# The last 224 features of gate and up with x stationary, and their way to the partitions through 32x32 transposes and DRAM

## The chip, the cores and the metric

The kernel runs on one core of a Trainium2 chip. The metric is device time in microseconds for one execution. The engines are PE (TensorE: matmuls; PEld are its weight loads), DVE (VectorE), ACT (ScalarE), POOL (GpSimd) and SP (SyncE, which here issues all DMAs). One profiled execution gives the trace that the text reads.

## What is computed

For 2048 tokens x of width 512, in float32:

```python
g = sigmoid((x * gate_w).sum(-1, keepdims=True))
a = sliding_window_attention(x @ wqkv, heads=32, head_dim=16, window=256) @ wo
b = (sigmoid(x @ w_gate) * (x @ w_up)) @ w_down        # 1376 features
out = g * a + (1 - g) * b
```

The change touches `x @ w_gate` and `x @ w_up` for the last 224 of the 1376 features, and the sum in `g`, which is computed as one more column of the same products.

## The kernel before

Every product of float32 values is made of three fp32r matmuls: each operand is split into a high part (an ACT cast) and a low part (a DVE subtraction), and high x high, high x low and low x high are added up in PSUM. x lies transposed in SBUF for the whole first phase (`xh`, `xl`: 512 inputs as 4 blocks of 128 partitions, 2048 tokens along the row).

**First phase, up to about 582 us.** A loop over 128 units (8 head groups of 4 heads x 16 query blocks; `u`) runs attention: score matmuls for the row maxima (`s_part`, L305; DVE finds the maximum, L311), transposed scores (`st_part`, L351; ACT takes the exponential, L356; POOL masks), and the product with V (`pv_part`, L384). PE has time to fill between them, and fills it with projections and with gate and up. The gate and up work is a list of groups, `rest`. Before, one group is (feature chunk f, weight w, token chunk c): the weights of 128 features are stationary, 512 tokens move, 12 matmuls (4 input blocks x 3 products), and the result has features on partitions. There are 11 chunks (ten of 128, one of 96), 2 weights, 4 token chunks: 88 groups. The 96 features of the last chunk take the gate's vector along as a 97th column in w=0.

The groups are not issued one by one. `turns()` (L527) cuts each matmul into two row halves of 64 partitions: in one turn it issues half 0 of matmul t and half 1 of matmul t-18, usually of another group, side by side on PE. Three turns go behind each head's score matmuls. When the second half of a group is through, its `post` goes to the front of the list `acts`, one entry of which is issued with each head: before, `gu_post` (L476), an ACT copy from PSUM to a staging tile `sp` (L479), whose store to the DRAM tensor `gu_d` is queued in `later` and issued by SP in the next unit (L279). The PSUM tiles of gate, up and projections share three buffers (tag `misc`). The last three groups are kept back (`HOLD`) and issued whole, with all 128 rows, around the end of the loop.

**Second phase, from about 582 us.** Four slices of 512 tokens, 11 steps each (`steps`, one per feature chunk). `h_load` (L549) brings gate and up of a step back from DRAM to one of eight buffers, five steps ahead; `h_skew` (L554) applies the sigmoid (ACT, L564) and the product (DVE, L565) three steps ahead and the split into `hb` (L67, L68; four buffers) two steps ahead; PE multiplies by `w_down` (`pd`, L71 to L73, 12 matmuls a step). In between, attention's output is loaded (`o_load`, L719 and L720), scaled and split; at the end of a slice PE applies `wo` (`pa`), DVE adds both parts with the gate's weights (L777), and SP stores the rows (L780). `gsum`, the argument of the gate's sigmoid, is gathered from `gu_d` by one DMA (L691) between the phases.

The order on PE, ACT, SP and DVE is the order of the code. Of the lines themselves, the ones that the working needs most:

```python
def gu_post(f, c, w):
    ...
    nc.scalar.copy(t[0:width(f, w)], gp.pop((f, c, w))[0:width(f, w)])
    later.append((gu_d[w, f, 0:fw, c * CH:(c + 1) * CH], t[0:fw]))
```

Of the kernel before, what the change touches and what calls it, by code (L numbers as in the profile page):

```python
# [22 lines left out]
CH = 512  # L23
NC = T // CH
NB = T // P
F = 1376
FCH = [P] * (F // P) + ([F % P] if F % P else [])
NF = len(FCH)
VW = DH + 1
# [9 lines left out]
QB = 32  # L39
HOLD = 3  # L40
GAP = 3
SHIFT = 18
WD_LATE = {0: 8, 1: 9, 2: 10}
# [5 lines left out]
def gated_mix_kernel(  # L49
# [28 lines left out]
    gu_d = nc.dram_tensor("gu_scratch", (2, NF, P, T), F32, kind="Internal").ap()  # L78
# [40 lines left out]
    with ExitStack() as actx:  # L119
# [114 lines left out]
        def group_mm(pt, fw, wh, wl, c, k, half):  # L234
            d, w = divmod(k, 2) if k < 2 * ND else (k - 2 * ND, 2)
            r = slice(0, P) if half is None else slice(64 * half, 64 * half + 64)
            mm(pt[0:fw], (wl if w == 2 else wh)[r, d], (xl if w == 1 else xh)[r, d, c * CH:(c + 1) * CH],  # L237
               start=k == 0 and half != 1, stop=k == 3 * ND - 1 and half != 0,
               skip_group_check=half is not None)

        def proj_mm(s, k, half=None):
            g, c = divmod(s, NC)
            if s not in pj:
                pj[s] = ps.tile([P, CH], F32, tag="misc", name=f"pj{s}", bufs=3)
            group_mm(pj[s], P, *wq[g], c, k, half)
# [197 lines left out]
        def gu_half(raw, fw):  # L443
            return raw.rearrange("p (d f) -> p d f", d=ND)[:, :, 0:fw]

        def width(f, w):
            return FCH[f] + (f == NF - 1 and w == 0)

        raw_gu = {}

        def load_gu(f, w):
            raw_gu[f, w] = cpool.tile([P, D], F32, tag="draw", name=f"guraw{f}_{w}", bufs=2)
            src = wgu[f, w] if FCH[f] == P else wgu_tail[w, :, :, 0:width(f, w)]
            nc.sync.dma_start(gu_half(raw_gu[f, w], width(f, w)), src)
# [3 lines left out]
        def split_gu(f, w):  # L458
            fw = width(f, w)
            raw = gu_half(raw_gu.pop((f, w)), fw)  # L460
            hi, lo = gv[:, 0, w, :, 0:fw], gv[:, 1, w, :, 0:fw]
# [8 lines left out]
        def gu_mm(f, c, w, k, half=None):  # L470
            fw = width(f, w)
            if (f, c, w) not in gp:
                gp[f, c, w] = ps.tile([P, CH], F32, tag="misc", name=f"gu{f}_{c}_{w}", bufs=3)
            group_mm(gp[f, c, w], fw, gv[:, 0, w, :, 0:fw], gv[:, 1, w, :, 0:fw], c, k, half)

        def gu_post(f, c, w):  # L476
            fw = FCH[f]
            t = cpool.tile([P, CH], F32, tag="sp", name=f"sp{f}_{c}_{w}", bufs=4)
            nc.scalar.copy(t[0:width(f, w)], gp.pop((f, c, w))[0:width(f, w)])  # L479
            later.append((gu_d[w, f, 0:fw, c * CH:(c + 1) * CH], t[0:fw]))  # L480
            if width(f, w) > fw:
                later.append((gu_d[w, f, fw:fw + 1, c * CH:(c + 1) * CH], t[fw:fw + 1]))
            if f + 1 < NF and c == 0:
                load_gu(f + 1, w)

        def gu_next(f, c, w):
            if f + 1 < NF and c == NC - 1:
                split_gu(f + 1, w)

# [4 lines left out]
        def proj_out(s):  # L494
# [10 lines left out]
            for f in range(NF) for w in range(2) for c in range(NC)  # L505
# [43 lines left out]
        def h_load(n):  # L549
            c, f = steps[n]  # L550
            for w in range(2):
                nc.sync.dma_start(hv[0:FCH[f], n % 8, w], gu_d[w, f, 0:FCH[f], c * CH:(c + 1) * CH])
# [44 lines left out]
        for u in range(N):  # L597
# [20 lines left out]
            if WD <= u < WD + 16 and (u - WD) % 2 == 0:  # L618
                load_d((u - WD) // 2)
            s4 = {5: 5, 9: 6, U_LAST: NSTEP - 2, U_LAST + 1: NSTEP - 1}.get(u)  # L620
# [45 lines left out]
            if 0 <= u - LAG < NU:  # L666
                mask_p(u - LAG)
            if WD + 2 <= u < WD + 18 and (u - WD) % 2 == 0:
                acts.append(lambda f=(u - WD) // 2 - 1: split_d(f, True))
# [21 lines left out]
        nc.sync.dma_start(gsum, gu_d[0, NF - 1, FCH[NF - 1]].rearrange("(b p) -> p b", p=P))  # L691
# [95 lines left out]
def _layout(inputs):  # L787
# [7 lines left out]
    nf = F // P  # L795
    gu = np.stack([wg, wu]).reshape(2, ND, P, F)
    main = gu[..., :nf * P].reshape(2, ND, P, nf, P).transpose(3, 0, 2, 1, 4)
    tail = gu[..., nf * P:].transpose(0, 2, 1, 3)
    gate = np.asarray(inputs["gate_w"]).reshape(1, ND, P, 1).transpose(0, 2, 1, 3)
    tail = np.concatenate([tail, np.broadcast_to(gate, (2, P, ND, 1))], axis=3)  # L800
# [32 lines left out]
```

## Time and profile before

| | us |
|---|---|
| median of 3 runs | 753.11 (752.37 to 753.42) |
| the profiled execution | 751.81 |
| its span, first to last instruction | 750.1 |
| PE, PEld busy | 744.0, 581.5 |
| DVE, ACT busy | 482.0, 435.5 |
| POOL busy | 171.9 |
| DMA moved | 103.58 MB in 69959 packets |

The granted PE clock is full throughout. A row of the timeline has start, duration, engine, line, operation and output<-inputs; a row of the windows has the stretch, its length, then busy time and number of instructions of PE, PEld, DVE, ACT and POOL, the clock, the mean busy share of the 16 DMA engines and GB/s; a row of the groups has count, busy time, mean ns of one, and the engine's idle time ahead of it with what ended it.

### The profile page before, as it was taken

What the parts mean: (1) busy time and instruction counts of PE and PEld (TensorE: products, weight loads), DVE (VectorE), ACT (ScalarE), POOL (GpSimd) and SP (SyncE); (2) the same over time, 40 slices, a digit from 0 to 9 for tenths busy, and PEclk for the clock granted to TensorE, in tenths of its full rate; (3) what the DMA queues carried; (4) which work ended last, traced back from release to release, by engine and by line L of the source; (5) the groups of instructions that cost most, each with busy time, mean ns of one, the idle gap of its engine ahead of it and who ended that gap; (6) DMA issues with size and microseconds to landing.
All of it is one profiled execution on the core that took longest, in us unless ns stands there. A gap on an engine that the chain in (4) does not pass through costs nothing.

```text
span 750.1 us, 17420 instructions
## 1 busy us (share of the span) xinstructions
PE 744.0 (99%) x6180; PEld 581.5 (78%) x6180; DVE 482.0 (64%) x1455; ACT 435.5 (58%) x927; POOL 171.9 (23%) x256
## 2 busy tenths in 40 slices
PE   8999999999999999999999999999999999999997
PEld 6877777787777877778787787778866888888886
DVE  5346767776776766776677676677613776657371
ACT  6422666666676667666667666666656663525241
POOL 7000233233233233323323333332331000000000
PEclk9999999999999999999999999999999999999999
DMA  8340434426344353443543426443355967557451
GB/s 305 96 113 19 105 98 124 127 68 181 113 114 125 109 154 105 122 112 108 153 122 92 125 71 177 125 130 102 109 187 176 290 209 233 170 194 223 128 150 56
DMA packets 69959, 103.58 MB, mean 138 GB/s; under 512 B 19314, under 2 KB 29042, under 8 KB 69872
## 3 DMA queue, kind: packets, MB, share of 16 engines
q1 hardware_dynamic: 69872, 102.48, 46.3%
q8 instruction: 48, 0.79, 0.4%
q14 instruction: 39, 0.32, 0.2%
HBM read 45.26 MB, written 32.00 MB: 103 GB/s over the span
## 4 chain that ended last, share of the span: by engine, by line
PE 97%; DMA 1%; DVE 1%; issue 0%; SPq 0%; ACT 0%; DVEq 0%
PE gu L237 34%; PE pv L384 12%; PE pj L237 11%; PE s L305 7%; PE st L351 5%; PE pd L71 5%; PE pd L73 5%; PE pd L72 5%; PE vps L71 2%; PE pa L73 2%; PE pa L71 2%; PE pa L72 2%; PE vps L73 2%; PE vps L72 2%; DMA V<-in_xT_dram 1%; DVE junk L311 0%
## 5 line engine op out<-in xcount | busy, mean ns | idle before, releaser
L311 DVE CUSTOM_DVE_ANT_0 junk<-s,mask 128x384 f32<-128x384 f32 (+2 forms) x512 | 272.1, 531 | 140.1 <-PE s L305 78.2
L237 PE MATMUL gu<-xh,w 64*128 64x512 f32 (+2 forms) x1384 | 344.4, 392 | 0.0
L356 ACT ACTIVATE pt<-st 128x384 f32<-128x384 f32 (+2 forms) x512 | 242.4, 474 | 169.3 <-PE st L351 69.8
L237 PE MATMUL gu<-xl,w 64*128 64x512 f32 (+3 forms) x692 | 227.4, 392 | 0.0
L237 PEld LDWEIGHTS gu<-xh,w 64*128 64x128 f32 (+2 forms) x1384 | 190.1, 183 | 19.3 <-issue 0.4
L361 POOL TENSOR_SCALAR_AFFINE_SELECT pt<-pt 128x512 f32<-128x512 f32 x128 | 88.1, 688 | 382.3 <-ACT pt L356 382.3
L351 PE MATMUL st<-ring 64*128 64x384 f32 (+2 forms) x536 | 170.2, 332 | 0.0
L305 PE MATMUL s<-ring 64*128 64x384 f32 (+2 forms) x536 | 165.8, 332 | 0.1
L305 PEld LDWEIGHTS s<-ring 64*128 64x128 f32 x536 | 94.4, 184 | 39.3 <-DVE nm L321 12.9
L237 PEld LDWEIGHTS gu<-xl,w 64*128 64x128 f32 (+3 forms) x692 | 107.9, 183 | 5.7
L351 PEld LDWEIGHTS st<-ring 64*128 64x128 f32 x536 | 97.1, 184 | 12.2 <-issue 2.7
L237 PE MATMUL pj<-xh,wqh 64*128 64x512 f32 (+1 forms) x232 | 91.1, 397 | 0.3 <-ACT xh L67 0.2
L384 PE MATMUL pv<-pt,V 128*32 128x384 f32 (+2 forms) x1408 | 91.0, 388 | 0.0
L237 PE MATMUL pj<-xl,wqh 64*128 64x512 f32 (+1 forms) x232 | 90.1, 393 | 0.4 <-DVE xl L68 0.4
L366 POOL TENSOR_SCALAR_AFFINE_SELECT pt<-pt 128x512 f32<-128x512 f32 x112 | 74.2, 663 | 0.0
L237 PE MATMUL pj<-xh,wql 64*128 64x512 f32 (+1 forms) x232 | 70.9, 392 | 0.0
L71 PE MATMUL pd<-ring,hb 128*128 128x512 f32 (+1 forms) x176 | 69.3, 394 | 0.0
L73 PE MATMUL pd<-ring,hb 128*128 128x512 f32 (+1 forms) x176 | 68.9, 392 | 0.0
L72 PE MATMUL pd<-ring,hb 128*128 128x512 f32 (+1 forms) x176 | 68.4, 389 | 0.0
L384 PEld LDWEIGHTS pv<-pt,V 128*32 128x32 f32 x1408 | 37.2, 109 | 36.0 <-issue 29.7
L67 ACT CAST hb<-V 128x512 fp32r<-128x512 f32 (+1 forms) x44 | 27.4, 622 | 63.9 <-DVE V L565 51.4
L479 ACT COPY sp<-gu 128x512 f32<-128x512 f32 (+2 forms) x88 | 51.1, 582 | 2.0 <-PE gu L237 2.0
(74 smaller groups left out, 898.5 us busy)
## 6 DMA issues: line engine op xcount, KB each, us to landing
gu_scratch<-sp SPq DMA_DIRECT2D x80, 256.0 KB
V<-gu_scratch SPq DMA_DIRECT2D x80, 256.0 KB
ring<-sh SPq DMA_DIRECT2D x128, 128.0 KB
ring<-sl SPq DMA_DIRECT2D x64, 128.0 KB
guraw<-in_wgu_dram SPq DMA_DIRECT2D x20, 256.0 KB
V<-in_xT_dram SPq DMA_DIRECT2D x16, 256.0 KB
oT_scratch<-ob SPq DMA_DIRECT2D x128, 32.0 KB
xl<-oT_scratch SPq DMA_DIRECT2D x16, 256.0 KB
```

Of the source, the lines that this page charges most:

```text
L71: mm(ps, lh, rh, start=first, stop=False)
L72: mm(ps, lh, rl, start=False, stop=False)
L73: mm(ps, ll, rh, start=False, stop=last)
L237: mm(pt[0:fw], (wl if w == 2 else wh)[r, d], (xl if w == 1 else xh)[r, d, c * CH:(c + 1) * CH], start=k == 0 and half != 1, stop=k == 3 * ...
L305: mm(pt[:, (k - k0) * P:(e - k0) * P], lhsT, blk(g, k, hh, 1, e - k), start=k == k0, stop=e == i + 1, skip_group_check=True,)
L311: nc.vector.tensor_tensor_reduce(junk[:, 0:n], pt[:, 0:n], mask[:, 3 * P - n:], scale=1.0, scalar=NEG, op0=ALU.add, op1=ALU.max, accum_out ...
L351: mm(pt[:, (q - j) * P:(e - j) * P], lhsT, blk(g, q, hh, 0, e - q), start=q == j, stop=e == last, skip_group_check=True,)
L356: nc.scalar.activation(pts[u][:, hh, 0:n], pt[:, 0:n], AF.Exp, scale=SCALE)
L361: nc.gpsimd.affine_select(p[:, :, 0:P], p[:, :, 0:P], pattern=[[0, HG], [1, P]], compare_op=ALU.is_ge, fill=0.0, base=0, channel_multiplie ...
L366: nc.gpsimd.affine_select(p[:, :, 2 * P:], p[:, :, 2 * P:], pattern=[[0, HG], [-1, P]], compare_op=ALU.is_gt, fill=0.0, base=0, channel_mu ...
L384: mm(pv[32 * hh:32 * hh + 32, (q % 4) * P:(q % 4 + e - q) * P], V[:, j, h * VW:h * VW + 32], p[:, hh, (q - j) * P:(e - j) * P], start=Fals ...
L479: nc.scalar.copy(t[0:width(f, w)], gp.pop((f, c, w))[0:width(f, w)])
```

## The change

The last two chunks (128 + 96 features) are taken out of the old scheme. Their gate and up weights stand side by side: 224 gate columns, 224 up columns, the gate's vector and a column of zeros, 450 in all. For each of 16 blocks of 128 tokens, x of that block is stationary and the 450 columns move (`tail_mm`), 12 matmuls a block. So `rest` has 9 x 2 x 4 = 72 old groups and 16 new ones: 88 as before, in the same places of the order, and with the same halves, turns and three held groups.

The result has tokens on partitions. `tail_post` transposes its 448 columns in 32x32 blocks on DVE, from PSUM to the staging tile, copies the gate's column straight to `gsum` on DVE, and queues one store. After a block transpose, partition 32a+j, column 32k+t holds token 32a+t, feature 32k+j; the store writes rows of 32 floats (128 bytes) to `tail_d`, 128 x 14 rows in one DMA. `h_load` of steps 9 and 10 reads them back with one DMA for each 32 features and weight, 32 partitions x 16 rows of 128 bytes each: 8 DMAs for step 9 and 6 for step 10, where there were 2 and 2.

The new weights come in four loads of 128x450 (u = 112, 114, 116, 118) through the `wqraw` buffers and are split two units later each, into two buffers of the projection weights and two of the four `hb` buffers. The last two chunks' old loads and splits go, and so does the gather of `gsum`.

```diff
+        def tail_room():
+            for k in range(2):
+                tw.append([
+                    wq_pool.tile([P, ND, P], F32R, tag=t, name=f"tail_{t}{k}").rearrange("p d f -> p (d f)")
+                    for t in ("wqh", "wql")
+                ])
+            for k in range(2):
+                both = cpool.tile([P, CH2], F32R, tag="hb", name=f"tail_hb{k}", bufs=4)
+                tw.append([both[:, 0:CH], both[:, CH:]])
...
+        def tail_mm(b, k, half=None):
+            if b not in tp:
+                tp[b] = ps.tile([P, CH], F32, tag="misc", name=f"tp{b}", bufs=3)
+            d, w = divmod(k, 3)
+            r = slice(0, P) if half is None else slice(64 * half, 64 * half + 64)
+            mm(tp[b][:, 0:TW], (xl if w == 1 else xh)[r, d, b * P:(b + 1) * P], tw[d][int(w == 2)][r, 0:TW],
+               start=k == 0 and half != 1, stop=k == 3 * ND - 1 and half != 0,
+               skip_group_check=half is not None)
+
+        def tail_post(b):
+            t = cpool.tile([P, CH], F32, tag="sp", name=f"tt{b}", bufs=4)
+            nc.vector.transpose(t[:, 0:2 * TF], tp[b][:, 0:2 * TF])
+            nc.vector.tensor_copy(gsum[:, b:b + 1], tp.pop(b)[:, 2 * TF:2 * TF + 1])
+            later.append((
+                tail_d[:, b].rearrange("k p t -> p k t"),
+                t[:, 0:2 * TF].rearrange("p (k t) -> p k t", t=QB),
+            ))
...
-            for f in range(NF) for w in range(2) for c in range(NC)
+            for f in range(NFM) for w in range(2) for c in range(NC)
+        ] + [
+            (lambda k, h=None, b=b: tail_mm(b, k, h), lambda: None, lambda b=b: tail_post(b)) for b in range(NB)
         ]
...
             for w in range(2):
-                nc.sync.dma_start(hv[0:FCH[f], n % 8, w], gu_d[w, f, 0:FCH[f], c * CH:(c + 1) * CH])
+                if f < NFM:
+                    nc.sync.dma_start(hv[:, n % 8, w], gu_d[w, f, :, c * CH:(c + 1) * CH])
+                    continue
+                for k in range(FCH[f] // QB):
+                    src = tail_d[(w * TF + (f - NFM) * P) // QB + k, c * NC:(c + 1) * NC]
+                    nc.sync.dma_start(
+                        hv[k * QB:(k + 1) * QB, n % 8, w].rearrange("j (m t) -> j m t", t=QB),
+                        src.rearrange("b (a j) t -> j (b a) t", j=QB),
+                    )
...
-        nc.sync.dma_start(gsum, gu_d[0, NF - 1, FCH[NF - 1]].rearrange("(b p) -> p b", p=P))
```

More of the change, by code (lines that the diff above doesn't have):

```diff
@@ L480, in gu_post @@
[L480 to L483, printed above, removed]
+            nc.scalar.copy(t, gp.pop((f, c, w)))
+            later.append((gu_d[w, f, :, c * CH:(c + 1) * CH], t))
+            if f + 1 < NFM and c == 0:
                 load_gu(f + 1, w)
         def gu_next(f, c, w):
-            if f + 1 < NF and c == NC - 1:
+            if f + 1 < NFM and c == NC - 1:
@@ new lines, in tail_load, with tail_split @@
+        def tail_load(d):
+            raw_gu[d] = cpool.tile([P, D], F32, tag="wqraw", name=f"tailraw{d}", bufs=2)
+            nc.sync.dma_start(raw_gu[d][:, 0:TW], wgu_tail[d])
+        def tail_split(d):
+            raw = raw_gu.pop(d)[:, 0:TW]
+            hi, lo = (v[:, 0:TW] for v in tw[d])
+            nc.scalar.copy(hi, raw)
+            behind.append(lambda: nc.vector.tensor_tensor(lo, raw, hi.bitcast(F32), op=ALU.subtract))
+        def tail_mm(b, k, half=None):
[6 more added lines that the diff above has]
+               skip_group_check=half is not None)
@@ L619, in gated_mix_kernel @@
                 load_d((u - WD) // 2)
+            if u == TAIL:
+                tail_room()
+            if TAIL <= u < TAIL + 2 * ND and u % 2 == 0:
+                tail_load((u - TAIL) // 2)
             s4 = {5: 5, 9: 6, U_LAST: NSTEP - 2, U_LAST + 1: NSTEP - 1}.get(u)
```

43 lines of the change are left out of this document (21 added, 22 removed).

## The prediction

> **What bounds the kernel now.** I read the profile's first part (busy time of each engine) and the chain that ended last, then the windows around the place of the change, then the order of single instructions there.
>
> ```profile
> span 750.1 us, 17420 instructions
> PE 744.0 (99%) x6180; PEld 581.5 (78%) x6180; DVE 482.0 (64%) x1455; ACT 435.5 (58%) x927; POOL 171.9 (23%) x256
> PE 97%; DMA 1%; DVE 1%; issue 0%; SPq 0%; ACT 0%; DVEq 0%
> ```
>
> PE is busy for 744.0 of 750.1 us, and 97% of the chain is PE. A busy PE alone would not prove much, because the ends of matmuls are modelled; so the distance between starts has to show whether PE runs tightly.
>
> ```profile
> 407.06 0.33 PE L351 MATMUL st<-ring 64*128 64x384 f32 x1
> 407.06 0.33 PE L305 MATMUL s<-ring 64*128 64x384 f32 x1
> 407.23 0.39 PE L237 MATMUL gu<-xh,w 64*128 64x512 f32 x1
> 407.23 0.39 PE L237 MATMUL gu<-xl,w 64*128 64x512 f32 x1
> ...
> 407.93 0.34 PE L351 MATMUL st<-ring 64*128 64x384 f32 x1
> ```
>
> Between the `st` at 407.06 and the one at 407.93 stand one pair of 384 columns (0.17 us, two row halves side by side) and three pairs of 512 columns (0.70 us, 0.233 each). The starts follow the number of moving columns, with no hole. So what a matmul streams is paid for in full, and DVE, ACT and DMA are bounds only where they make PE wait. The windows show where they come near:
>
> ```profile
> 508.00:540.00 32.00, 32.00 (x335) 25.53 (x333) 22.34 (x77) 21.13 (x48) 9.79 (x15) 1.00 0.33 103
> 540.00:582.00 42.00, 42.00 (x356) 29.43 (x353) 11.23 (x19) 26.23 (x61) 10.13 (x16) 1.00 0.59 181
> 582.00:610.00 28.00, 28.00 (x124) 22.98 (x123) 24.50 (x43) 18.82 (x35) 0.00 (x0) 1.00 1.01 305
> 623.00:664.00 41.00, 41.00 (x181) 33.64 (x181) 24.90 (x42) 17.78 (x30) 0.00 (x0) 1.00 0.60 191
> ```
>
> The columns are PE, PEld, DVE, ACT, POOL, clock, DMA share, GB/s. The last 16 groups of gate and up run from about 508 to 582. DVE has 9.7 us free before 540 and plenty after it; at 582 to 610 (the first slice of the second phase) the DMA engines are full, and DVE is busy for 24.5 of 28 us.
>
> **Matmuls: the gain.** Before, the last two feature chunks take 2 chunks x 2 weights x 4 token chunks x 12 = 192 matmuls of 512 moving columns (a pair of row halves counts as one). After, 16 token blocks x 12 = 192 matmuls of 450 columns, with as many weight loads. The first 18 turns, whose other half still belongs to chunk 8, stay at the pace of 512; at the end 18 turns with one half alone gain, so 192 remains the count. The price of 62 columns comes from the starts: (0.233 - 0.17) / 128 = 0.49 ns a column. A second pair of rows gives less:
>
> ```profile
> 567.37 0.28 PE L351 MATMUL st<-ring 64*128 64x256 f32 x1
> 567.49 0.39 PE L237 MATMUL gu<-xh,w 64*96 64x512 f32 x1
> 567.72 0.39 PE L237 MATMUL gu<-xl,w 64*96 64x512 f32 x1
> ```
>
> A single 256 takes 0.12, a single 512 takes 0.23: 0.43 ns a column. So 62 columns are worth 27 to 30 ns; the second row crosses a shorter distance of unlike neighbours, and I take 27: 192 x 0.027 = **5.2 us saved**. The ends are 0 (if something else set the pace) and 192 x 0.0305 = 5.9. That weight loads could set the pace is ruled out as far as 0.17: the 384 pairs load two stationary operands of 128 columns each, as the new matmuls do. The Trainium skill (TensorE: Matmul & The Clock Gate, section "Wait — 56ns, not 53.3ns?") says that start-to-start is the columns over 2.4 GHz plus about 2.5 ns; by that 62 columns are 25.8 ns and the gain 5.0 us. The trace has 0.233 where that rule has 0.216, so its fixed part is larger here, and its slope a little smaller than my rows give.
>
> **DVE instead of ACT: the cost.** 16 ACT copies go, 16 DVE transposes of 128x448 and 16 DVE copies of one column come.
>
> ```profile
> L311 DVE CUSTOM_DVE_ANT_0 junk<-s,mask 128x384 f32<-128x384 f32 x448 | 249.4, 557 | 118.2 <-PE s L305 64.5 <-PE st L351 43.0 <-PE gu L237 0.2
> L479 ACT COPY sp<-gu 128x512 f32<-128x512 f32 x80 | 46.5, 581 | 0.0
> L727 DVE STREAM_SHUFFLE spare<-xh 128x512 f32<-128x512 f32 x16 | 11.7, 733 | 0.0
> L326 DVE STREAM_TRANSPOSE nt<-nm 128x32 f32<-128x32 f32 x32 | 6.8, 211 | 1.1
> L715 DVE TENSOR_SCALAR omg<-gs 128x16 f32<-128x16 f32 x1 | 0.2, 169 | 0.0
> ```
>
> No row has a wide transpose. Lower bound: one block, 0.21 us (L326); upper: 14 such instructions, 2.95 us. I take the line between L326 and the shuffle of 512, which also moves 32-row blocks: 211 + (733 - 211) x 416 / 480 = 663 ns; the copy of one column at most 169 ns: 0.83 us a block, 13.3 us in all. ACT loses 16 x 0.58 = 9.3 us, which buys nothing, since ACT is no bound there.
>
> How much of it PE sees: three PSUM buffers serve these groups, and the first matmul of group n waits until group n-3 has been read. By the order of the instructions this lies some seven turns behind: three of the 384 pairs and six new pairs, 3 x 0.17 + 6 x 0.206 = 1.75 us. Until 540 DVE must first take the maximum of the next score tile (0.56 + 0.08, beginning about 0.3 after its matmul), in one case a 0.27 memset too, then transpose and copy: 0.3 + 0.64 + 0.83 = 1.8 to 2.05 us. That is 0 to 0.3 us late for each of groups 1 to 3; group 0 has the PV matmuls in between, and from 540 on DVE has no maxima left. What queues behind a late transpose is the next maximum, and behind that the PE matmul that needs its score buffer. I put **0.5 us** on this. The ends are 0 and, with 2.95 us transposes, about 1.3 to 2.3 us for each of 13 groups, 25 us in all; near 0.66 is where the shuffle row lies.
>
> The four splits of the new weights replace four splits of the old ones on the same engines (0.6 us each), some 20 us earlier, where DVE idles a third of each step; nothing. Two of the four `hb` buffers now hold weights until the last group, so step 2 of the second phase can be split only from the phase's start. It is needed two steps (5.5 us) later and takes about 3 us with the last two transposes ahead of it: nothing.
>
> **DMA: the pieces of 128 bytes.** Each of 16 stores becomes 1792 packets of 128 B instead of 128 or 96 of 2 KB, and per slice 14 loads of 512 packets replace 4 loads. Two windows hold small packets nearly alone: the stores of the maxima (128 packets of 128 B, and 64 semaphore packets), and the gather of `gsum` (4 B each), which the change removes. The third is one 256 KB output store.
>
> ```profile
> DMA packets 192, 0.02 MB, mean 10 GB/s; under 512 B 192, under 2 KB 192, under 8 KB 192
> q1 hardware_dynamic: 192, 0.02, 7.8%
> ...
> DMA packets 1630, 0.03 MB, mean 33 GB/s; under 512 B 1617, under 2 KB 1617, under 8 KB 1630
> q1 hardware_dynamic: 1630, 0.03, 97.4%
> ...
> q1 hardware_dynamic: 144, 0.26, 53.7%
> ```
>
> 7.8% of 16 engines over 1.7 us is 2.1 us for 192 packets, 11 ns each; 97.4% over 1.0 us is 9.6 ns each; 53.7% over 1.3 us is 11.2 us, 0.70 us on each engine. So a new store takes about 1808 x 11 / 16 = 1.24 us of the engines against 0.70, every 3.5 to 4 us, in windows with shares of 0.33 and 0.59: hidden. A slice's 14 loads take 14 x 528 x 11 / 16 = 5.1 us against 4 x 0.70 = 2.8. No row reads 128 B pieces from HBM; the bounds are 5.5 ns (the 2 KB rate) and, from the 4 B reads, hardly over 10, and I keep three times as a rival.
>
> SP's queue is the tighter place:
>
> ```profile
> 584.18 0.45 SPq L691 DMA_DIRECT2D gsum<-gu_scratch  x1
> 584.68 2.97 SPq L552 DMA_DIRECT2D V<-gu_scratch  x2
> ...
> 596.09 2.50 SPq L552 DMA_DIRECT2D V<-gu_scratch  x4
> 598.95 0.38 SPq L719 DMA_DIRECT2D xl<-oT_scratch  x1
> ...
> 604.46 3.18 SPq L552 DMA_DIRECT2D V<-gu_scratch  x6
> 615.50 8.48 SPq L780 DMA_DIRECT2D out_dram<-spare  x4
> ...
> 632.39 1.74 SPq L552 DMA_DIRECT2D V<-gu_scratch  x4
> ...
> 640.50 3.05 SPq L552 DMA_DIRECT2D V<-gu_scratch  x6
> 656.64 8.49 SPq L780 DMA_DIRECT2D out_dram<-spare  x4
> ```
>
> The loads of the last two chunks are the x4 at 596.09 and 632.39. With 0.43 to 0.5 us an issue (1.74 / 4, and the 512-packet load of 0.38 plus its gap), 14 of them take 6.6 us: 4 to 5 us more in each slice. SP then idles less before the output stores (607.6 to 615.5 and 643.6 to 656.6), which hides it from the end. What moves back are the loads queued behind: `xl`, and the next slice's first steps. From the second slice on, PE's data stand ready several steps ahead. In the first they don't:
>
> ```profile
> 596.65 0.68 DVE L68 TENSOR_TENSOR hb<-V,hb 128x512 fp32r<-128x512 f32 x1
> ...
> 604.08 0.69 DVE L68 TENSOR_TENSOR hb<-V,hb 128x512 fp32r<-128x512 f32 x1
> ...
> 606.67 0.68 DVE L68 TENSOR_TENSOR hb<-V,hb 96x512 fp32r<-96x512 f32 x1
> ```
>
> These ready steps 6, 9 and 10. PE begins step n at 581.6 + 2.75 n (12 x 0.229), that is 598.1, 606.3 and 609.1: slack 0.8, 1.5 and 1.7 us. Step 9's eight loads end their issue 1.3 us later than its two did (4 x 0.63 before, 8 x 0.47 after), step 10's 4 us later, part of which the emptier DMA queue gives back. Against this, the `gsum` gather goes; after it the next load took until 587.7 for two issues, some 2 us more than usual, though the two last stores will now hold SP for part of that. I put 0.5 us on the first slice (ends 0, since PE doesn't wait there today, and 4).
>
> **Sum.** -5.2 + 0.5 + 0.5 = -4.2 us. The profiled execution took 751.81 with a span of 750.1; it would be 747.6. It lies 1.3 below the median of the runs shown, 753.1, for which the forecast is **748.9**.
>
> **Rivals.** (1) *DVE eats the gain.* Transposes near 1 us, or a longer wait in the queue, make PE late by about 1 us at each of groups 1 to 3 and cost another 1 us: -5.2 + 4 = about 752. For: DVE's maxima and the new work fill nearly all of a step before 540. Against: subtractions of 0.69 stand in the same queue today and leave no hole in PE's starts. (2) *Small pieces cost three times as much* (33 ns). This is the one that ends slower. A slice's loads take 15 us of the engines; in the first slice, where they are full, step 9 and 10 come some 12.5 - 1.6 = 11 us late, and in each other slice (14 x 1.1 us of issue and landing from 632.4, data wanted near 646) about 2: -5 + 11 + 6 = +12, about 765. It decides from about twice the 11 ns, where the first slice's stall equals the gain. Against it: the 11 and 9.6 ns above. The Trainium skill (DMA: Bandwidth & Descriptors, section "Rules for kernel authors") speaks against a transpose by a plain DMA with a rearranged pattern, 19 times slower than the transposing kind; no run here shows it, and here 128 B stay together. (3) *The matmuls don't get shorter*, because something beside the columns sets 0.23: then only the costs stay, 753 to 754. Against it stand 0.17 and 0.12.
>
> **Chances.** The forecast's case 0.72 (747.0 to 751.3), rival 1 0.11, rival 2 0.12 (anything from 753 up), rival 3 0.05. The range 747.0 to 753.0 leaves out most of 2 and 3 and the top of the gain. A measurement of this kernel can tell about 0.2%, 1.5 us. Faster than 751.6: 0.72 plus a part of rival 1, 0.75; within it: 0.12; slower than 754.6: 0.13.
>
> **What would show it.** Right: starts of the 450 matmuls 0.20 to 0.21 apart; transposes near 0.66; the first matmul of the second phase 4 to 5 us before 581.6; step distances of 2.75 after it. Wrong: PE idle before the first matmul of a group, released by a transpose (rival 1); ACT or DVE in steps 9 and 10 waiting for loads, with PE behind them (rival 2); pairs at 0.23 (rival 3).

## The result, and the profile after

The changed kernel takes 759.78 us (median of 6 runs, 759.41 to 760.72), the kernel before 752.74 beside it (6 runs). The ratio is 1.0093 [1.0079, 1.0107]: 7.0 us slower, where 4.2 us faster was forecast. The profiled execution took 759.82. Executions of one kernel differ by up to 5 us here, and a profile shows one of them, so its own time is given where it lies far from the median.

The first part, DMA totals and chain of the profile after:

```profile
span 758.0 us, 17531 instructions
...
PE 744.6 (98%) x6180; PEld 585.0 (77%) x6180; DVE 491.4 (65%) x1487; ACT 427.0 (56%) x911; POOL 171.2 (23%) x256
...
DMA packets 121519, 103.57 MB, mean 137 GB/s; under 512 B 74206, under 2 KB 84446, under 8 KB 121432
...
PE 91%; DMA 4%; DVE 2%; SPq 1%; ACT 1%; issue 1%; DVEq 0%; ACTq 0%
```

PE's busy time is hardly changed, but its share of the chain fell from 97 to 91%: DMA, DVE and SP have come into it. The number of packets grew from 69959 to 121519 for the same 103.6 MB. The windows say where; their columns are those of the prediction's:

```profile
508.00:540.00 32.00, 31.92 (x344) 26.80 (x340) 24.54 (x85) 19.57 (x45) 9.87 (x16) 1.00 0.38 94
540.00:577.00 37.00, 36.84 (x340) 28.79 (x338) 14.45 (x35) 19.19 (x46) 9.64 (x16) 1.00 0.84 189
577.00:610.00 33.00, 29.70 (x124) 22.61 (x123) 22.79 (x43) 16.53 (x30) 0.00 (x0) 1.00 0.83 206
610.00:620.00 10.00, 6.74 (x17) 4.65 (x17) 8.20 (x14) 6.20 (x12) 0.00 (x0) 0.66 0.80 265
620.00:664.00 44.00, 44.00 (x194) 36.15 (x193) 25.43 (x43) 19.14 (x34) 0.00 (x0) 1.00 0.64 178
```

Up to 577 and from 620 on PE is full. All of the loss lies from 577 to 620, in the first slice of the second phase; between 610 and 620 the granted clock, too, is down at 0.66. The first matmul of that phase stands on either side of it. After:

```profile
577.59 0.36 PE L512 MATMUL tp<-tail_hb,xh 128*128 128x450 f32 x1
577.79 0.39 PE L75 MATMUL pd<-ring,hb 128*128 128x512 f32 x1
```

Before:

```profile
581.44 0.40 PE L71 MATMUL pd<-ring,hb 128*128 128x512 f32 x1
```

So the first phase **did** become 3.65 us shorter. The first slice then takes 52.6 us instead of 41.2, **11.4 longer**; the three other slices keep their 41.2. -3.65 + 11.4 = +7.75, and the spans differ by 7.9. The starts of the steps of the first slice are normally 2.75 apart (the last, with `wo`, takes 13.68); after, steps 4 to 6 take 4.20, 3.79 and 3.29 (3.0 us too much), and steps 8 to 10 take 3.94, 6.81 and 16.85 (8.4 too much).

What SP issued meanwhile (rows of SP's queue; start, time in which the issues held SP, xcount issues):

```profile
580.85 1.31 SPq L737 DMA_DIRECT2D spare<-in_wo_dram  x3
...
582.74 2.73 SPq L284 DMA_DIRECT2D tail_scratch<-tt  x2
585.52 2.12 SPq L590 DMA_DIRECT2D V<-gu_scratch  x2
...
596.55 9.87 SPq L594 DMA_DIRECT2D V<-tail_scratch  x14
...
607.69 1.81 SPq L590 DMA_DIRECT2D V<-gu_scratch  x4
```

The 14 loads hold SP for 9.9 us where four held it for 2.5, and two stores of 1792 pieces hold it for 2.7. The first load of the *next* slice's step 0 stands behind them: it goes out at 607.69, against 600.08 before, 7.6 us later. Before:

```profile
600.08 2.39 SPq L552 DMA_DIRECT2D V<-gu_scratch  x4
```

That this matters to the present slice is seen on ACT,

```profile
609.04 0.62 ACT L71 CAST hb<-V 96x512 fp32r<-96x512 f32 x1 [1.53 <-DVE V L610]
612.37 0.63 ACT L609 ACTIVATE V<-V 128x512 f32<-128x512 f32 x1 [2.70 <-DMA V<-gu_scratch]
612.90 0.60 ACT L116 CAST ring<-wdraw 96x512 fp32r<-96x512 f32 x1
```

and on PE:

```profile
610.05 0.39 PE L77 MATMUL pd<-ring,hb 128*128 128x512 f32 x1
613.56 0.80 PE L75 MATMUL pd<-ring,hb 96*128 96x512 f32 x1 [3.12 <-ACT ring L116]
614.49 0.79 PE L76 MATMUL pd<-ring,hb 96*128 96x512 f32 x1
```

What PE waits for longest is the last chunk of `w_down` (the low part of step 10's own `h` is ready at 611.98). The chunk was issued at 592.46, but its split (L116) stands on ACT behind the sigmoid (L609) of the next slice's step 0, which waits for the load that SP issued behind the 14. After 3.5 us without a start the first matmul takes 0.80, and from 615.1 to about 619.4 the starts stand 0.43 apart, not 0.23.

The stretch before 577, for the steps of the prediction. Starts of the 450-column pairs (one row half each):

```profile
528.93 0.36 PE L512 MATMUL tp<-tail_wqh,xh 64*128 64x450 f32 x1
...
529.13 0.36 PE L512 MATMUL tp<-tail_wqh,xl 64*128 64x450 f32 x1
...
529.34 0.36 PE L512 MATMUL tp<-tail_wql,xh 64*128 64x450 f32 x1
```

They are 0.20 apart, and a step between two score matmuls takes 0.78 where it took 0.87: 0.09 for three matmuls, 30 ns each. All transposes and all one-column copies (smallest, median and largest of the 16 in ns), as the two lines' own views have them:

```profile
L518 DVE STREAM_TRANSPOSE tt<-tp x16: 616/644/650, 520.5 to 581.1; 128x448 f32<-128x448 f32 x16
```

```profile
L519 DVE COPY gsum<-tp x16: 118/119/122, 521.0 to 581.7; 128x1 f32<-128x1 f32 x16
```

And one of the places where a group waited for them, first DVE's rows, then PE's:

```profile
530.53 0.27 DVE L406 MEMSET pv<- 128x256 f32 x1
530.71 0.62 DVE L518 STREAM_TRANSPOSE tt<-tp 128x448 f32<-128x448 f32 x1
531.25 0.12 DVE L519 COPY gsum<-tp 128x1 f32<-128x1 f32 x1
```

```profile
531.10 0.33 PE L356 MATMUL st<-ring 64*128 64x384 f32 x1
...
531.52 0.44 PE L512 MATMUL tp<-tail_wqh,xh 64*128 64x450 f32 x1
```

The new group begins 0.41 after the score matmul, not 0.17, behind memset, transpose and copy.

### The profile page after: what moved, and what is told of

It reads as the page before. It is cut to its first block, busy times and chain, and to the rows that moved or that the text cites. A ratio compares the mean times of both kernels' runs of the same rounds, so it can differ in the third digit from the quotient of the medians.

```text
span 758.0 us, 17531 instructions
## 1 busy us (share of the span) xinstructions
PE 744.6 (98%) x6180; PEld 585.0 (77%) x6180; DVE 491.4 (65%) x1487; ACT 427.0 (56%) x911; POOL 171.2 (23%) x256
## 2 busy tenths in 40 slices
DMA packets 121519, 103.57 MB, mean 137 GB/s; under 512 B 74206, under 2 KB 84446, under 8 KB 121432
## 4 chain that ended last, share of the span: by engine, by line
PE 91%; DMA 4%; DVE 2%; SPq 1%; ACT 1%; issue 1%; DVEq 0%; ACTq 0%
PE gu L242 27%; PE pv L389 11%; PE pj L242 10%; PE s L310 8%; PE st L356 5%; PE tp L512 5%; PE pd L77 4%; PE pd L76 4%; PE pd L75 4%; PE vps L75 2%; PE pa L75 2%; PE pa L77 2%; PE pa L76 2%; PE vps L76 2%; PE vps L77 2%; DMA V<-in_xT_dram 1%
## 5 line engine op out<-in xcount | busy, mean ns | idle before, releaser
L242 PE MATMUL gu<-xh,w 64*128 64x512 f32 x1152 | 295.1, 392 | 0.0
L242 PE MATMUL gu<-xl,w 64*128 64x512 f32 x576 | 190.5, 392 | 0.0
L242 PEld LDWEIGHTS gu<-xh,w 64*128 64x128 f32 x1152 | 160.6, 184 | 14.5
L242 PEld LDWEIGHTS gu<-xl,w 64*128 64x128 f32 x576 | 90.6, 185 | 3.8
L75 PE MATMUL pd<-ring,hb 128*128 128x512 f32 (+1 forms) x176 | 70.6, 401 | 4.8 <-ACT ring L116 3.1
L77 PE MATMUL pd<-ring,hb 128*128 128x512 f32 (+1 forms) x176 | 70.4, 400 | 1.6 <-DVE hb L72 1.6
L76 PE MATMUL pd<-ring,hb 128*128 128x512 f32 (+1 forms) x176 | 69.6, 396 | 0.1
L242 PEld LDWEIGHTS pj<-xl,wqh 64*128 64x128 f32 (+1 forms) x232 | 42.4, 185 | 4.3 <-DVE xl L72 1.9
```

What stands on the lines that cost most here:

```text
L75: mm(ps, lh, rh, start=first, stop=False)
L76: mm(ps, lh, rl, start=False, stop=False)
L77: mm(ps, ll, rh, start=False, stop=last)
L242: mm(pt, (wl if w == 2 else wh)[r, d], (xl if w == 1 else xh)[r, d, c * CH:(c + 1) * CH], start=k == 0 and half != 1, stop=k == 3 * ND - 1 ...
```

## The experiments

The theory after the result (COUNT): SP's row of issues is what became late; 14 loads for 4, and stores whose many pieces hold the queue. Its rivals: the small pieces cost DMA engine time; PE itself comes too early for loads that cannot come earlier; and, for the missing part of the gain, VectorE or a smaller price of columns. "First slice" below is its excess over the 41.2 us of before, in the profiled execution, worked out from the starts of the `pd` matmuls; "phase one" is the time from the same hole in PE's starts near 506 to the first `pd` (before 75.46, after 71.80).

**1. Loads by whole rows.** The tail's loads are 4 DMAs of 2 KB rows in a slice; stores as in the change.

```diff
-                for k in range(FCH[f] // QB):
-                    src = tail_d[...]
-                    nc.sync.dma_start(hv[k * QB:(k + 1) * QB, n % 8, w]..., src...)
+                nc.sync.dma_start(hv[0:FCH[f], n % 8, w], flat[off:off + FCH[f] * CH]...)
```

> The changed kernel, but steps 9 and 10 load the same number of bytes of the scratch tensor as whole rows of 2 KB, one DMA for each weight (4 a slice in place of 14 of 128-byte pieces); which values arrive is not the feature order, so the output is not the reference's. Theory COUNT (SP issues 14 DMAs at about 0.5 us, and everything behind them comes late) and theory PIECES (packets of 128 bytes fill the DMA engines in a stretch where they are full already) both expect the 8.4 us of steps 8 to 10 of the first slice to go, and about 751.5 us. Theory EARLY (the first slice's loads can't come earlier with PE, so that the first phase's gain is lost there) expects the 3.0 us of steps 4 to 6 to stay. If both are wrong, it stays near 759.8.

Measured: 753.22, ratio 1.0007 [0.9997, 1.0016]; first slice +4.9: steps 4 to 6 still 2.5, steps 8 to 10 2.4. The loads are worth 6.6 us; the 2.5 of steps 4 to 6 have another source.

**2. Fourteen loads, but of rows.** 14 DMAs of 32 x 2 KB.

```diff
+                for k in range(FCH[f] // QB):
+                    nc.sync.dma_start(hv[k * QB:(k + 1) * QB, n % 8, w], flat[o:o + QB * CH]...)
```

> As the run with whole rows, but cut into 14 DMAs a slice (32 partitions, 2 KB each), so that the count is that of the changed kernel and the pieces are long; the values are again not in feature order. COUNT expects about the changed kernel, 757 to 760; PIECES expects 751 to 752, as with 4 DMAs.

Measured: 758.59, 1.0066 [1.0041, 1.0090]; first slice +10.0 (step 9 takes 6.72). With the pieces gone and the count kept, 5.4 of the 6.6 us are back, by the medians: count 5.4, pieces 1.2. The five times lie between 754.52 and 759.65, so the 1.2 is not clear of the scatter; that the count is the larger part is.

**3. Stores by rows as well.** Experiment 1 with each block stored as 128 rows of 1792 bytes.

```diff
-                tail_d[:, b].rearrange("k p t -> p k t"),
-                t[:, 0:2 * TF].rearrange("p (k t) -> p k t", t=QB),
+            later.append((flat[o:o + 2 * TF * P].rearrange("(p x) -> p x", x=2 * TF), t[:, 0:2 * TF]))
```

> As the run with whole rows, and the 16 stores too are rows (128 of 1792 bytes in place of 1792 of 128); values not in feature order. If the stores of small pieces held SP up at the end of the first phase, steps 4 to 6 of the first slice lose most of their 3.0 us: about 749. EARLY expects them to stay, 751 to 752.

Measured: 749.76, 0.9962 [0.9948, 0.9977]; first slice +1.6, steps 4 to 6 normal. SP at the end of the first phase with small stores (experiment 1):

```profile
579.75 1.31 SPq L735 DMA_DIRECT2D spare<-in_wo_dram  x3
...
581.64 3.21 SPq L284 DMA_DIRECT2D tail_scratch<-tt  x2
584.89 2.12 SPq L590 DMA_DIRECT2D V<-gu_scratch  x2
```

and with row stores:

```profile
578.81 1.31 SPq L734 DMA_DIRECT2D spare<-in_wo_dram  x3
...
581.37 0.92 SPq L284 DMA_DIRECT2D tail_scratch<-tt  x2
582.34 1.34 SPq L589 DMA_DIRECT2D V<-gu_scratch  x2
```

Two stores of 1792 pieces hold SP for 3.2 us, two of 128 pieces for 0.9, and step 5's loads go out 2.5 us earlier. This is what made steps 4 to 6 late: by 2.5 us in experiment 1, by 3.0 in the change. PE enters the second phase as early here (578.0) as in the changed kernel, so coming early is no cost of its own: that rival falls.

**4. The count alone, on the kernel before.** Its loads of steps 9 and 10 are cut into 14 DMAs of 32 rows of 2 KB; nothing else.

```diff
+                for k in range(FCH[f] // QB):
+                    nc.sync.dma_start(
+                        hv[k * QB:(k + 1) * QB, n % 8, w],
+                        gu_d[w, f, k * QB:(k + 1) * QB, c * CH:(c + 1) * CH],
+                    )
```

> The kernel before with one edit: the loads of steps 9 and 10 are cut into 14 DMAs of 32 partitions a slice, in rows of 2 KB as before. COUNT alone, without anything else of the change: the first slice has 1.5 us of slack at step 9, 14 issues take some 4 to 5 us more, so COUNT expects 3 to 8 us more, 756 to 761. PIECES and EARLY expect no difference, 752.7.

Measured: 758.05, 1.0071 [1.0052, 1.0090]; first slice +5.5. SP, then PE:

```profile
597.54 8.23 SPq L556 DMA_DIRECT2D V<-gu_scratch  x14
...
607.00 1.82 SPq L553 DMA_DIRECT2D V<-gu_scratch  x4
```

```profile
609.46 0.39 PE L73 MATMUL pd<-ring,hb 128*128 128x512 f32 x1
612.50 0.50 PE L71 MATMUL pd<-ring,hb 96*128 96x512 f32 x1 [2.65 <-ACT ring L111]
```

Ten more issues a slice, without any other part of the change, bring the same hole at the same place: PE waits for the split of `w_down`.

**5. The split ahead of the sigmoid.** The changed kernel with one order turned round on ACT and DVE.

```diff
+            if n in WD_SPLIT:
+                split_d(WD_SPLIT[n])
             h_skew(n)
             if n in WD_LATE:
                 load_d(WD_LATE[n])
-            if n in WD_SPLIT:
-                split_d(WD_SPLIT[n])
```

> The changed kernel with one thing turned round: in each step of the second phase the split of a w_down chunk (steps 4, 6 and 8) is issued ahead of that step's sigmoid and splits of h instead of behind them. The count of loads (14 in a slice) and the stores stay. Theory ORDER (the 3.5 us hole of PE ahead of step 10 is the w_down split of chunk 10, which stands on ACT behind a sigmoid that waits for a load queued behind the 14): the hole goes, with it the about 2 us of half clock after it; the split of h for step 10 still comes late, so step 9 is not normal; 754 to 756. Rival LOADS ALONE (step 10's own data come so late that PE would wait as long for them): 758.5 to 760. Steps 4 to 6 keep their 3 us in both.

Measured: 755.72, 1.0032 [1.0021, 1.0044]: by the medians some 4 us of the loss are this queueing, as ORDER had it. The profiled execution took 757.80 (the nine: 754.51 to 757.80), and its first slice is still +8.8. The hole ahead of step 10 is smaller in it, but not gone: a start-to-start of 1.9 us, now for DVE's half of the same split (L117), which stands behind work that waits for a load. Half clock follows it from 615.2 to 618.7.

```profile
613.00 0.50 PE L76 MATMUL pd<-ring,hb 96*128 96x512 f32 x1 [1.47 <-DVE ring L117]
```

The other waits of the slice (3.4 us) are for the splits of `h`, and so for the loads themselves.

**6. ACT copies in place of the transposes,** on experiment 3.

```diff
-            nc.vector.transpose(t[:, 0:2 * TF], tp[b][:, 0:2 * TF])
-            nc.vector.tensor_copy(gsum[:, b:b + 1], tp.pop(b)[:, 2 * TF:2 * TF + 1])
+            nc.scalar.copy(t[:, 0:TW], tp.pop(b)[:, 0:TW])
+            nc.scalar.copy(gsum[:, b:b + 1], t[:, 2 * TF:2 * TF + 1])
```

> The run with row stores and row loads (749.76, second phase from 578.0), with the 16 transposes of 128x448 and the 16 copies of one column on VectorE replaced by two ACT copies each from PSUM, as the kernel before has them; nothing is transposed, so the features go into the wrong places. Theory VECTORE IN THE WAY: the 1.5 us that are missing between the 5.2 us of shorter matmuls and the 3.65 us by which the second phase begins earlier are waits of groups for the transposes; with ACT copies the second phase begins near 576.5 and the time is 748.0 to 748.6. Rival SHORTER GAIN (62 columns are worth less than 27 ns, some 19 to 20): the second phase still begins at 577.8 to 578.2, and the time stays 749.5 to 750.

Measured: 748.88, 0.9939 [0.9927, 0.9951], but not by the expected way: phase one takes 72.40, no shorter than with transposes (71.84), and in the profiles what is gained is the 1.6 us of the first slice. Now `st` waits for an exponential four times (PE's waits from 505 to 577):

```profile
PE st L356 <- ACT pt L361: 1.0, 4, 0.3
```

VECTORE IN THE WAY falls as I put it: taking the work off DVE doesn't bring the 1.5 us, since ACT's queue then holds PE as often. SHORTER GAIN falls too, since 62 columns are worth 30 ns, not 20. In experiment 3 the first slice's 1.6 us are a wait at step 10 for DVE's half of the `w_down` split, which runs at 606.51 there and at 605.24 here, while PE came to the second phase 0.5 us earlier there. Why it runs later there, with `wo` loaded at 578.8 in both, stays open.

**7. The same 14 loads from POOL's queue.**

```diff
-                    nc.sync.dma_start(
+                    nc.gpsimd.dma_start(
                         hv[k * QB:(k + 1) * QB, n % 8, w].rearrange("j (m t) -> j m t", t=QB),
```

> The changed kernel with nothing but the queue of the 14 tail loads of a slice changed: POOL issues them instead of SP, with the same pieces of 128 bytes and the same count. Theory SP QUEUE (what was late was SP's row of issues, at most 8 at a time, and all loads behind the 14): the holes of steps 8 to 10 shrink from 8.4 us to at most those of the run with row loads (1.4 to 2.4); steps 4 to 6 stay 3 us late, since the stores are untouched: 753 to 755. Rival DMA ENGINES (14 loads with 7168 pieces are too much for the full DMA engines, whoever issues them): 758 or more. A third way is that POOL's issue of one such load takes much longer than SP's 0.45 us; then steps 9 and 10 come late for that, in this slice above all.

Measured: 757.73, 1.0051 [1.0033, 1.0069]. Steps 8 to 10 are 2.9 us late, not 8.4: same pieces, same count, another queue. But steps 4 to 6 are now 5.9 us late, not 3.0. POOL issues the first of the loads from 579.0 on, 17.6 us before SP had come to them in the changed kernel (596.55). So they are on the DMA engines together with `wo`, the last stores and the loads of step 5; SP's two stores hold it for 3.51 us,

```profile
583.00 3.51 SPq L284 DMA_DIRECT2D tail_scratch<-tt  x2
```

and the first load of step 5 lands at 592.5, not at 590.4. The theory is nearly right for steps 8 to 10 (at most 2.4 were expected) and wrong on the total: loads that go out early push back the ones that are wanted first.

**8. Stores in quarters, loads of rows.** Features lie in DRAM row by row: each block is stored by four DMAs of 32 partitions with pieces of 128 bytes, and loaded as before the change.

```diff
+            for a in range(P // QB):
+                o = b * P + a * QB
+                later.append((
+                    tail_d[:, o:o + QB].rearrange("(k j) t -> j k t", j=QB),
+                    t[a * QB:(a + 1) * QB, 0:2 * TF].rearrange("j (k t) -> j k t", t=QB),
+                ))
```

> The transposed features lie in DRAM feature by feature (448 rows of 2048 tokens): a token block is stored by four DMAs, one for each 32 partitions, each 32 x 14 rows of 128 bytes, and a step is loaded as before the change, by two DMAs of whole 2 KB rows. Theory COUNT ON SP: the loads take no time of their own any more, so the end of the first slice is as in the run with row loads (steps 8 to 10 near 3.6, 3.1, 14.9), and the last stores, now 4 DMAs instead of 1 for each block, hold SP at the end of the first phase at least as long as there (steps 4 to 6 late by 3 us or up to 2 more): 753 to 755.5. Rival FIRST PHASE (64 stores instead of 16 make SP late while attention still runs, and PE waits for staging tiles or for rows of the stack): the second phase begins later than 579.5, 756 or more.

Measured: 759.32, 1.0078 [1.0064, 1.0092]: a miss, as FIRST PHASE had it. Steps 8 to 10 lose only 1.1 us, but the 64 stores hold SP at the end of the first phase: a chunk of `w_down` goes out at 577.10 (the same one at 571.24 in the changed kernel), ACT waits 4.0 us for it, and PE behind ACT:

```profile
581.14 0.50 PE L75 MATMUL pd<-ring,hb 128*128 128x512 f32 x1 [3.63 <-ACT hb L71]
```

**9. Small stores not last.** Experiments 5 and 8 together, and the last four old groups put behind the 16 new ones (their weights are loaded 6 units earlier).

```diff
+        rest = rest[:-NB - NC] + rest[-NB:] + rest[-NB - NC:-NB]
```

> As the one with stores in quarters, and two more edits: the four last groups of the old kind (chunk 8, w=1) go behind the 16 new ones, so that the last stores of the first phase are single DMAs of 2 KB rows again (the new weights are loaded 6 units earlier for that), and the w_down splits stand ahead of the sigmoids. Theory COUNT ON SP: nothing of the first slice is late any more, the second phase begins near 578, all steps are 2.75 and 13.68: 748.5 to 750, below the kernel before. Rival FIRST PHASE: the 64 small stores cost PE time before 578, or the earlier weights wait for their buffers: 752 or more.

Measured: 752.13, 0.9988 [0.9978, 0.9998]; phase one 72.97, first slice +2.1. Better than both kernels, against the one before by a hair, but a miss: the time is what FIRST PHASE gave, and phase one has lost 1.2 us to the changed kernel. `wo` is loaded at 581.40, 2.6 us later than in experiment 3: SP is still late.

**10. All 64 quarters from POOL,** on experiment 9 (`nc.gpsimd.dma_start` in place of `later.append`).

> The reordered version (four last old groups behind the new ones, w_down splits first, features stored by quarters, whole rows loaded; 752.1), with its 64 quarter stores issued by POOL instead of SP. Theory SP QUEUE: SP is back to the issues of the kernel before at the end of the first phase, less the gather, so wo and the first loads come about 2.5 us earlier than in that run, steps 0, 6 and 8 are near 2.75, and the time is 749.0 to 750.5. Rival POOL IN THE WAY (64 issues on POOL delay its masks, or the stores land late): the second phase begins later than 579.5, 752 or more.

Measured: 753.83, 1.0007 [0.9991, 1.0022], a miss, as POOL IN THE WAY. The profiled execution took 756.95 (the twelve: 752.44 to 756.95). In it the first slice has no late step, but the second phase begins at 586.3; 6.8 us before it, from 571.4 to 578.2, run at half clock. At full clock it would begin near 583, an estimate from these two. POOL's groups from 510 to 590:

```profile
L524 POOL DMA_DIRECT2D tail_scratch<-tt x60 | 37.7, 635 | 10.7 <-DVE gsum L521 3.9 <-issue 3.0 <-DVE mx L316 1.6
L366 POOL TENSOR_SCALAR_AFFINE_SELECT pt<-pt 128x512 f32<-128x512 f32 x17 | 11.5, 675 | 1.2 <-ACT pt L361 1.2
```

An issue takes POOL 0.635 us, 38 us of it in all, and the masks behind them come late: PE waits 1.20 us for one at 571.26. SP's row is cured, and POOL's is in the way instead.

**11. Stores and loads of the change from POOL** (one store a block, 14 loads a slice, split first).

> The changed kernel's layout (one store of a block with pieces of 128 bytes, 14 loads a slice), order of groups as in the change, w_down splits first, with both the 16 stores and the 14 loads of a slice issued by POOL. Theory SP QUEUE: neither the stores nor the loads stand in SP's row; the second phase begins near 578, steps 4 to 6 are normal, 8 to 10 late by at most 2 us: 749.5 to 751.5. Rival DMA ENGINES: steps 8 to 10 still several us late, 754 or more.

Measured: 777.96, 1.0322 [1.0298, 1.0346], outside both expectations. POOL gets through one large store in some 6.6 us:

```profile
599.39 1.10 POOL L520 DMA_DIRECT2D tail_scratch<-tt  x1 [6.26 <-issue]
605.95 1.10 POOL L520 DMA_DIRECT2D tail_scratch<-tt  x1 [5.45 <-DVE spare L777]
```

so the loads behind them land late, and step 8 takes 16.1 us. The landings in the trace say what POOL waits for: its next issue begins 0.3 us after the store ahead of it has landed (605.65 and 605.95, 612.24 and 612.54). Small ones overlap: up to three loads of 512 pieces are under way at once.

**12. Only the last four blocks' quarters from POOL,** on experiment 8 with the split first.

```diff
+                if b < NB - NC:
+                    later.append((dst, src))
+                else:
+                    nc.gpsimd.dma_start(dst, src)
```

> The version with stores in quarters and whole rows loaded (759.3; order of groups as in the change), with the w_down splits ahead of the sigmoids, and the stores of the last four token blocks issued by POOL instead of SP; POOL's last mask comes before the first of these. In the run where POOL issued all 64, one issue took 0.63 us, the masks came late and the second phase began at 586.3, but no step after it was late. Theory SP QUEUE: with 16 of the 64 on POOL behind the masks, SP's row is shorter than before the change, the second phase begins at 577.5 to 578.5, no step is late: 747 to 749.5. Rival STILL LATE (the 48 stores before, or the POOL stores' landing, hold the loads of the first steps): steps 0 to 6 late by 2 us or more, 750.5 to 753.

Measured: 755.32, 1.0036 [1.0023, 1.0049]: a miss, and above the range of STILL LATE too. Steps 1 to 10 are normal, but the 48 stores before make SP late. A chunk of `w_down` that SP issued at 571.24 in the changed kernel goes out at 576.49 here and lands at 581.41. It

```profile
576.49 0.42 SPq L110 DMA_DIRECT2D wdraw<-in_wd_dram  x1
```

holds ACT,

```profile
581.44 0.62 ACT L116 CAST ring<-wdraw 128x512 fp32r<-128x512 f32 x1 [4.29 <-DMA wdraw<-in_wd_dram]
```

and through it step 0:

```profile
582.63 0.80 PE L75 MATMUL pd<-ring,hb 128*128 128x512 f32 x1 [4.76 <-ACT hb L71]
```

**13 and 14. One and two quarters of each block from POOL,** on experiment 9.

```diff
+                    nc.gpsimd if a >= 2 else nc.sync,
```

(In 13 the condition is `a == 3`.)

> The reordered version (752.1; stores by quarters, whole rows loaded, the four last old groups behind the new ones, w_down splits first), with one of the four quarter stores of each block issued by POOL, 16 of 64. In that run SP's row blocked twice for 1.1 us near 557 and 571 behind the stores, and the wo loads went out at 581.4 where the run with row stores and ACT copies had 578.8. Theory SP'S ROW BEFORE 575 sets when the second phase's loads start: with 16 issues of 0.5 us less on SP, wo is loaded 1 to 2 us earlier, the late steps 0, 6 and 8 lose 1 to 2 us in all: 750.3 to 751.3. Rival DMA ENGINES: the pieces of 128 bytes are the same, so wo and the late steps stay: 752 or more. POOL has room for one issue of 0.63 us between its masks; if it hasn't, the second phase begins later than 579.5.

> The same with two of the four quarter stores on POOL, 32 of 64. Theory SP'S ROW: SP has then no more issues than before the change; 749.3 to 750.5, unless POOL's masks come late (all 64 on POOL made the second phase begin at 586.3); then PE waits for masked tiles before 572 and the time is 751 to 753 in spite of an SP row that is on time. Rival DMA ENGINES: 752 or more with wo and the late steps as in the reordered version.

Measured: 750.49, 0.9956 [0.9939, 0.9972], and **749.45, 0.9947 [0.9930, 0.9964]**. In both profiles, every step of the second phase is at its 2.75 or 13.68. `wo` is loaded at 581.40 in experiment 9, at 578.63 with one quarter moved, and with two:

```profile
577.84 1.32 SPq L741 DMA_DIRECT2D spare<-in_wo_dram  x3
...
580.39 0.81 SPq L284 DMA_DIRECT2D gu_scratch<-sp  x2
```

The windows of the version with two quarters:

```profile
540.00:578.00 38.00, 37.84 (x338) 29.03 (x336) 13.85 (x30) 20.86 (x49) 19.52 (x32) 1.00 0.79 190
578.00:620.00 42.00, 42.00 (x186) 34.47 (x185) 31.14 (x55) 24.39 (x44) 0.00 (x0) 1.00 0.75 238
```

PE is full from 578 to 620. The second phase begins at 578.5; phase one takes 72.80, so 2.7 of the changed kernel's 3.65 us are kept. The pieces are the same as in experiment 9; only issues left SP. Theory SP'S ROW is borne out, and DMA ENGINES falls for what was left.

## Why the prediction was wrong, point by point

- **Matmuls, 5.2 us: right in kind, a little small.** 0.20 between starts, 30 ns a matmul instead of 27, so 192 x 0.030 = 5.8. The 25.8 ns of the Trainium skill's rule that the prediction named (TensorE: Matmul & The Clock Gate, section "Wait — 56ns, not 53.3ns?") is the farther one.
- **Transposes, 0.66 us: right** (0.644); the copy took 0.119, under its bound of 0.169.
- **Waits for them, 0.5 us: too small.** Phase one gained 3.65 of 5.8, so by difference waits took some 2.1 us; not each of them is located. One is shown above, by the mechanism named (memset, transpose, copy in one row). That they would end at 540 was wrong: PE's starts show the same 0.41 at 547.8 and 555.7, where DVE has a `w_down` split of 0.69 ahead of the transpose, and from 543 to 559 the gain is 0.58 us, half of what the pace of the 7 us before 527 would give. Experiment 6 speaks for the fixed order of two full queues as the cause, and not DVE alone: on ACT the same work costs PE as much.
- **The new weights' splits, nothing; the emptier ACT, nothing: no run speaks against it.**
- **The step that failed: "I put 0.5 us on the first slice (ends 0, since PE doesn't wait there today, and 4)".** It measured 11.4. The row was read rightly (14 issues, more in SP's row), and then priced by the two loads of steps 9 and 10 alone. Its own sum was off, too: step 9's two loads ended after 2 x 0.63 = 1.26 us of the row, not after 4 x 0.63, so eight of 0.47 end 2.5 us later, not 1.3, against a slack of 1.5. Three more things are missing in it. First, 14 issues held SP for 9.9 us, not 6.6: two of them took 1.77 and 1.38 us in place of 0.49, and three times the row stood, some 0.6 us in all, until an earlier DMA had landed (the issue of 598.39 began 0.02 us after the landing of the one eight before it, issued at 593.13). The issue of step 9's last load ended at 603.23, against 597.26 before. Secondly, "what moves back are the loads queued behind: `xl`, and the next slice's first steps" was taken to be harmless in this slice. But ACT takes its work in order, and the next slice's sigmoid stands ahead of this slice's last `w_down` split; experiment 5 puts about 4 us on that, half clock included. Thirdly, the prediction saw that "the two last stores will now hold SP for part of that" and charged nothing for it; experiment 3 shows 3.5 us for small stores against rows.
- **Rival 2 named the place and the sign, with the wrong mechanism.** A piece of 128 bytes took 13 to 14 ns of a DMA engine on average (the packets of the changed kernel from 520 to 576 and from 582 to 610), near the 11 of the sum and far from this rival's 33. The pieces are 1.2 us of the 6.6, not clear of the scatter (experiment 2); the count on one queue is the rest, and the count alone, on the old kernel, costs 5.2 us (experiment 4). The other slices lost nothing, against the 6 us that this rival put on them.
- **Rival 1 was half right, rival 3 is out.** The waits behind DVE took some 2.1 of the 4 us of rival 1, but with transposes of 0.644 us, and they leave a gain; the matmuls did get shorter.
- **The gain was real.** With the queue relieved, experiment 14 is 0.53% faster than the kernel before, about 4 us; the forecast for the change itself was 4.2. That the two numbers lie so close is partly luck: the sum behind 4.2 has 5.2 and 0.5 for what measured 5.8 and some 2.1, and in the two profiles the spans differ by 2.8 only (750.1 and 747.3).

The Trainium skill (DMA: Bandwidth & Descriptors, section "Issuing engines are not separate DMA queues") says that starting DMAs from several engines only saves the sequencer's time for the start, "usually small relative to the DMA itself". Experiment 7 agrees with the first half: from POOL's queue the same pieces still push other loads back. The second half holds here for one DMA (the load issued at 607.69 took 0.38 us to issue and landed at 612.35), not for a row of them: 32 of 64 stores moved from SP to POOL brought the `wo` loads out 3.6 us earlier and took 2.7 us off the median (experiments 9 and 14).

## What to carry to other kernels

When one DMA becomes several, count the issues in the row of the queue that carries them, and follow every load behind them to the instruction that waits for it, on engines that take their work in order, also where that instruction belongs to a later piece of work. Slack has to be read at each of these waiting instructions, not only at the one whose data the DMA brings. A gain that is there in one stage can be made good by moving some issues to a queue with room, as long as that queue's own work isn't pushed back.

## What the runs showed of the hardware

- SP has at most eight DMAs under way in this program: in every trace here no issue of SP begins before the DMA eight places ahead of it has landed, and in full rows it begins right after (592.46 after 592.40, 598.39 after 598.37 in the changed kernel). And issues last longer behind DMAs of many pieces: 3.21 us for two stores of 1792 pieces, 0.92 for two of 128 (experiments 1 and 3).
- After some holes PE runs at half its pace: 0.43 between starts from 615.1 to about 619.4 after the 3.5 us hole, with a granted clock of 0.66 from 610 to 620. So a hole can cost more than its length, here some 2 us more. The length of one hole doesn't decide it: half clock followed starts 3.04 us apart in experiment 4, 1.91 (at 613.00) in experiment 5 and 1.69 (at 571.26) in experiment 10, and none followed 2.12 us at 594.21 in experiment 5. The Trainium skill (TensorE: Matmul & The Clock Gate, section "Part 1: The HAM clock gate (the "warmup" mystery)") gives one idle window of about 3.4 us for that, and half the clock; the trace agrees on the half, and the holes here were in part shorter.
- An issue from POOL takes 0.64 us of its time for a store of 32 partitions, 0.65 for a load, and 1.1 us for a store of 1792 pieces (experiments 7, 10, 11). Of these stores and loads POOL never has more than 1792 pieces under way in these traces: one store of 1792, three loads of 512, or four stores of 448 (experiments 7, 10, 11 and 12).
